# Two global attention steps per batch: all eight heads on half of the keys each, instead of four heads on all keys

## The chip, the cores and the metric

The kernel runs on one core of one Trainium2 chip. The metric is the device time of one execution in microseconds (us), and lower is better. In the rows, PE is TensorE (PEld its weight loads), DVE is VectorE, ACT is ScalarE, POOL is GpSimd and SP is SyncE, which issues most transfers.

## The reference

Local and global attention, then a layer of one expert that takes the 128 highest-scoring tokens of each batch. Cut to what matters:

```python
batch, n_heads, seq_l, seq_g, head_dim = (8, 8, 512, 32, 64)
...
def sm(s):
    s = s - np.max(s, axis=-1, keepdims=True)
    e = np.exp(s)
    return e / (np.sum(e, axis=-1, keepdims=True) + 1e-09)
k_all = np.concatenate([k_g, k_l], axis=2)
v_all = np.concatenate([v_g, v_l], axis=2)
s_g = scale * np.matmul(q_g, k_all.transpose(0, 1, 3, 2))
out_g = np.matmul(sm(s_g), v_all)
...
mask = np.abs(pos[:, None] - pos[None, :]) <= window      # window = 32
s_l = np.concatenate([s_lg, s_ll], axis=-1)
out_l = np.matmul(sm(s_l), np.concatenate([v_g, v_l], axis=2))
x = np.concatenate([out_g, out_l], axis=2)                # to (B, 544, 512)
...
scores = np.einsum('bsd,d->bs', x, w_gate)
top_idx = np.argpartition(-scores[b], capacity)[:capacity]    # per batch
ye = np.maximum(xe @ w1, 0.0) @ w2                            # xe = x[b, top_idx]
out[b, top_idx] = x[b, top_idx] + g[:, None] * ye             # g = sigmoid(scores)
```

The change is in `s_g` and `out_g`: 32 global queries in each of 8 heads, against 544 keys, in each of 8 batches.

## The kernel before, in words

A batch is six steps, in the order L0, L1, G0, G1, L2, L3. A local step (L) takes 128 local queries of all eight heads against their windows of 128 keys. A global step (G) takes the 32 global queries of four heads against all 544 keys, so that heads times queries fill the 128 partitions. There are 48 steps, and one loop writes their instructions out; each engine runs its own list in that written order, so the order in the code is the order on the engine.

One turn of the loop, for step i, does the following.

- PE: for local steps `opened` of step i+1 (a matmul that writes the mask, L209); the attend matmuls of step i-1 (L284 for L, L378 for G); the score matmuls of step i+1 (L228 for L, L337 for G); the transposes of step i's probabilities (L267 for L, L368 for G); then a portion of the expert's matmuls, the fill (L510, L538, L554), whose size a planner sets.
- DVE: `attend_out` of step i-1 (L299, L301, L306 for L; L388, L390, L392 for G), the row maxima of step i+1 (L240 for L; L341, L342, L344 for G), the gate score of a finished tile (L323), then its share of the ranking of the batch before (L424, L426, L434, L436), one or two tiles of tokens per turn, and the second halves of the expert's products (L541).
- ACT: the copies of step i's transposed probabilities from PSUM to SBUF (`turned`, L272), then the scaling of step i+1's maxima (L248) and its exponentials (L258 for L, L352 for G), then the expert's copies and relus (L540).

So the exponentials of step i+1 follow its scores and maxima in the same turn, and its transposes come one turn later. In G steps the probabilities go to the tile `pg`, whose blocks that no key uses are zeroed once at the start. The score tiles `s_ps` are PSUM banks, two to a step, from a pool of six; a step's banks come free when `attend_out` has read the result.

Every matmul in float32 stands in the trace as two matmuls and two weight loads. Score matmuls use a quarter of the array's columns (32 queries) and half of its rows (64 of the head dimension): heads with an even index take rows 0 to 63, heads with an odd one rows 64 to 127. In L steps a row of the score tile is a chunk of 32 queries, and the two heads of a pair go to the two banks. In G steps before the change head h of four goes to columns 32h of the array, with rows 64 * (h % 2).

K, V and Q come by SP's queue: for each batch four tiles `v_t` (V of 128 local keys and their neighbours, two transfers each), `k_t` and `q_t` tiles, and stores of the result. A wait of SP holds what is written behind it. Each step's global result is written by one transfer of SP (L394), behind L392.

## Time and profile before

| | us |
|---|---|
| three runs, median | 345.84 |
| three runs, lowest and highest | 342.60 and 345.89 |
| the profiled execution | 338.32 |
| its span, first to last instruction | 336.1 |

| engine | busy share of the span |
|---|---|
| PE | 84% |
| PEld | 67% |
| DVE | 64% |
| ACT | 51% |
| POOL | 12% |

The profiled execution took 2.2 us outside its span. It is 7.5 us shorter than the median of the three runs; what is worked out from it is a difference in time, which is then put on the median. Busy shares are means over stages with different limits: the first 80 us also load the expert's weights, the middle is attention with fill, and the last 45 us are the expert's alone. TensorE's granted clock is at full speed (2.4 GHz) for 95% of the span by the mean, and at 1.2 GHz in single slices.

### The profile page before, as it was taken

To read this page: it belongs to the slowest core of one execution; us is meant where nothing else is said; L and a number is where in the kernel's file an instruction comes from. 1 tells how busy PE (TensorE), PEld (TensorE's weight loads), DVE (VectorE), ACT (ScalarE), POOL (GpSimd) and SP (SyncE) were. 2 spreads that over 40 slices of the span, in tenths; PEclk is the share of its full clock that TensorE was granted. 3 is DMA by queue.
4 is the path that set the end of the run, shared out by engine and by line. 5 is a ranking of instruction groups with operands and counts; after the bars stand their busy time and mean duration, and the time that the engine had idled before them with its cause. 6 is when DMAs were issued, how large, how long until landed. Compare 5 with 4: busy or idle time off the path is not lost.

```text
span 336.1 us, 14525 instructions
## 1 busy us (share of the span) xinstructions
PE 282.5 (84%) x6328; PEld 226.7 (67%) x6328; DVE 215.6 (64%) x673; ACT 173.0 (51%) x515; POOL 38.8 (12%) x38
## 2 busy tenths in 40 slices
...
GB/s 216 396 408 387 400 385 403 219 248 393 342 37 72 368 403 185 80 377 410 190 11 346 405 244 62 190 390 406 69 67 377 213 33 31 116 33 29 34 33 31
DMA packets 29951, 75.93 MB, mean 226 GB/s; under 512 B 5440, under 2 KB 9408, under 8 KB 29888
## 3 DMA queue, kind: packets, MB, share of 16 engines
...
q8 instruction: 50, 0.82, 1.0%
q10 hardware_dynamic: 288, 0.15, 0.2%
...
## 4 chain that ended last, share of the span: by engine, by line
PE 44%; issue 20%; DVE 13%; DMA 11%; ACT 8%; POOL 3%; SPq 1%; POOLq 0%; DVEq 0%; ACTq 0%
PE s_ps L284 8%; PE s_ps L267 6%; PE s_ps L228 6%; PE m_ps L554 6%; DMA v_t<-in_vw_dram 5%; PE m_ps L538 5%; ACT p_t L258 5%; PE s_ps L337 4%; DMA k_t<-in_kT_dram 4%; DVE mxl L240 3%; DVE junk L424 2%; PE s_ps L378 2%; DMA xe<-out_dram,ix 2%; PE s_ps L368 2%; DVE junk L426 2%
## 5 line engine op out<-in xcount | busy, mean ns | idle before, releaser
L272 ACT COPY pt<-s_ps 128x512 f32<-128x512 f32 (+1 forms) x96 | 50.5, 556 | 67.6 <-PE s_ps L267 34.0
L258 ACT ACTIVATE p_t<-s_ps,nb 128x128 f32<-128x128 f32 x256 | 69.5, 383 | 1.0
L284 PE MATMUL s_ps<-v_t,pt 128*32 128x65 f32 x2048 | 41.7, 231 | 15.1 <-issue 12.2
L284 PEld LDWEIGHTS s_ps<-v_t,pt 128*32 128x32 f32 x2048 | 34.4, 115 | 24.5 <-issue 17.6
L240 DVE TENSOR_REDUCE mxl<-s_ps 128x4 f32<-128x512 f32 x64 | 41.0, 682 | 10.8 <-PE s_ps L228 10.7
L228 PE MATMUL s_ps<-k_t,q_t 64*32 64x128 f32 x2048 | 41.8, 292 | 5.4 <-issue 2.7
L267 PE MATMUL s_ps<-cs,p_t 128*128 128x128 f32 x256 | 39.0, 295 | 3.6 <-issue 2.0
L228 PEld LDWEIGHTS s_ps<-k_t,q_t 64*32 64x32 f32 x2048 | 31.5, 112 | 10.2 <-issue 7.4
L267 PEld LDWEIGHTS s_ps<-cs,p_t 128*128 128x128 f32 x256 | 29.6, 150 | 11.2 <-issue 6.5
L299 DVE TENSOR_SCALAR den<-s_ps 128x4 f32<-128x4 f32 x64 | 9.1, 157 | 29.1 <-PE s_ps L284 25.3
L424 DVE SCALAR_TENSOR_TENSOR junk<-r,sc,side_w 128x128 bf16<-128x128 f32 (+4 forms) x40 | 24.7, 617 | 1.7 <-ACT r L412 0.2
L306 DVE TENSOR_TENSOR x<-s_ps,rec 128x256 f32<-128x256 f32 x64 | 24.2, 419 | 1.1
L323 DVE CUSTOM_DVE_ANT_0 junk<-x,wgb 128x512 bf16<-128x512 f32 x32 | 23.7, 741 | 0.1
L426 DVE SCALAR_TENSOR_TENSOR junk<-r,sc,side_w 128x544 bf16<-128x544 f32 (+4 forms) x40 | 22.4, 560 | 2.1 <-DMA q_t<-in_qT_dram 0.2
...
L561 POOL DMA_INDIRECT out_dram<-xe,ix x8 | 8.1, 1013 | 117.9 <-DVE recg L390 60.6
L248 ACT ACTIVATE nb<-mxl 128x8 f32<-128x8 f32 x32 | 6.9, 216 | 27.9 <-DVE mxl L240 27.8
L337 PE MATMUL s_ps<-k_t,qg_t 64*32 64x256 f32 (+1 forms) x384 | 20.3, 342 | 0.9 <-DMA qg_t<-in_qgT_dram 0.9
L554 PE MATMUL m_ps<-w2h,hTh 128*128 128x512 f32 x48 | 20.6, 429 | 0.2 <-DVE xe L559 0.2
L538 PE MATMUL m_ps<-xTh,w1h 128*128 128x256 f32 x76 | 19.8, 294 | 0.0
L541 DVE SCALAR_TENSOR_TENSOR hTl<-m_ps,hTh 128x256 fp32r<-128x256 f32 x19 | 8.0, 424 | 17.3 <-ACT hTh L540 17.3
L554 PE MATMUL m_ps<-w2l,hTh 128*128 128x512 f32 x48 | 19.1, 398 | 0.0
...
## 6 DMA issues: line engine op xcount, KB each, us to landing
...
```

Source lines behind the costliest of these rows:

```text
L228: nc.tensor.matmul(out=s_ps[hp][32 * j:32 * j + 32, P * pr:P * pr + P], lhsT=q_t[t // 2][rows, pr, 32 * (c % 8):32 * (c % 8) + 32], rhs=wi ...
L240: nc.vector.tensor_reduce(out=mx[:, NPAIR * hp:NPAIR * hp + NPAIR], in_=s_ps[hp].rearrange("p (r k) -> p r k", k=P), axis=AX.X, op=ALU.max)
L258: nc.scalar.activation(out=p_t[:, cc], in_=s_ps[hp][:, cc], func=AF.Exp, scale=0.125, bias=nb[:, k:k + 1])
L267: nc.tensor.transpose(s_ps[hp][:, cc], p_t[:, cc], ident)
L272: nc.scalar.copy(out=pt[:, 0:n], in_=s_ps[hp][:, 0:n])
L284: nc.tensor.matmul(out=s_ps[hp][32 * j:32 * j + 32, VD * pr:VD * pr + VD], lhsT=pt[:, x0:x0 + 32], rhs=v_t[:, j, NPAIR * hp + pr, :], star ...
L306: nc.vector.tensor_tensor(out=xt[b, t][:, :, hp], in0=o_ps[hp][:, :, 0:D], in1=rec[:, hp].broadcast_to([P, NPAIR, D]), op=ALU.mult)
L337: nc.tensor.matmul(out=s_ps[part][32 * h:32 * h + 32, c0:c1], lhsT=qg_t[rows, pr, :], rhs=r_, start=True, stop=True)
L424: nc.vector.scalar_tensor_tensor(out=junk[:n, 0:hi], in0=r[:n, 0:hi], scalar=s, in1=side_w[:n, P + SL - lo:P + SL - lo + hi], op0=ALU.is_g ...
L426: nc.vector.scalar_tensor_tensor(out=junk[:n, lo:ST], in0=r[:n, lo:ST], scalar=s, in1=side_w[:n, 0:ST - lo], op0=ALU.is_gt, op1=ALU.mult, ...
L538: nc.tensor.matmul(out=h_ps, lhsT=a[:, kc, ms], rhs=xT[x_][:, kc, :], start=(i == 0), stop=(i == len(prods) - 1))
L554: nc.tensor.matmul(out=y_ps, lhsT=hT[h_][:, mc, cc], rhs=w[:, mc, :], start=(part == 0 and i == 0), stop=(part == 3 and i == len(prods) - 1))
```

## The change

Each of the two G steps of a batch now takes all eight heads on half of the keys: step G0 takes 288 key columns, step G1 256. Heads of even index go to one bank (`hp` 0), of odd index to the other (`hp` 1), as in L steps. Each half has its own maximum, so the second step forms the minimum of the two scaled maxima, and a factor `gf` by which the first half's sum is rescaled; `oa` holds that sum in SBUF in between. G0 no longer divides or stores; G1 does it for all eight heads, with one transfer.

The tile `pg` is the same size, split by `hp`; a block that only G0 fills is zeroed by DVE in each G1 (L365 of the changed kernel). ACT has one more exponential, of `gf`, behind those of G1.

```diff
@@ -25,7 +25,6 @@
 NPAIR = H // 2
 NQ = H // 4
 VD = D + 1
-OG = 300
 KB = 3 * (NC // 2) + 2
 KW = 32 * KB
 KW1 = 448
@@ -61,10 +60,9 @@
 
 
 
-_GWIN = (0, 3, 6, 9, 12, 15)
-NGB = 4 * len(_GWIN)
-GH = (2, 4)
-GCOL = (((0, 256, 0),), ((0, 256, 384), (256, 288, 768)))
+GWIN = ((0, 3, 6), (9, 12, 15))
+GN = (288, 256)
+OG = 400
 
 
 @with_exitstack
@@ -146,10 +144,11 @@
                 return ps_s.tile([P, 512], FP32, name="s_ps")
         return ps_m.tile([P, 512], FP32, name="m_ps")
 
-    pg = cst.tile([P, NGB, 32], FP32, name="pg")
-    nc.vector.memset(pg[:, 0:8], 0.0)
-    nc.gpsimd.memset(pg[:, 8:], 0.0)
-    wz = pg[:, 0:8].rearrange("p n k -> p (n k)").bitcast(BF16)
+    pg = cst.tile([P, 2, 12, 32], FP32, name="pg")
+    nc.vector.memset(pg[:, 0, 0:8], 0.0)
+    nc.gpsimd.memset(pg[:, 0, 8:], 0.0)
+    nc.gpsimd.memset(pg[:, 1], 0.0)
+    wz = pg[:, 0, 0:8].rearrange("p n k -> p (n k)").bitcast(BF16)
     for i in range(WARM):
         w_ps = m_tile()
         nc.tensor.matmul(out=w_ps, lhsT=wz[:, 0:P], rhs=wz, start=True, stop=True)
@@ -234,7 +233,7 @@
 
     def maxima(g, s_ps):
         if g[1] == "G":
-            return g_max(s_ps)
+            return g_max(g[0], g[2], s_ps)
         mx = sm.tile([P, H], FP32, name="mxl")
         for hp in range(2):
             nc.vector.tensor_reduce(out=mx[:, NPAIR * hp:NPAIR * hp + NPAIR], in_=s_ps[hp].rearrange("p (r k) -> p r k", k=P),
@@ -250,7 +249,7 @@
 
     def expo(g, s_ps, nb, hp):
         if g[1] == "G":
-            return g_exp(s_ps[hp], nb, hp)
+            return g_exp(g[2], s_ps[hp], nb, hp)
         p_t = att.tile([P, 512], FP32, name=f"p_t{hp}")
         for pr in range(NPAIR):
             cc = slice(P * pr, P * pr + P)
@@ -268,14 +267,14 @@
 
     def turned(g, s_ps, hp):
         pt = att.tile([P, 512], FP32, name=f"pt{hp}")
-        n = GH[hp] * P if g[1] == "G" else 512
+        n = 3 * P if g[1] == "G" else 512
         nc.scalar.copy(out=pt[:, 0:n], in_=s_ps[hp][:, 0:n])
         return pt
 
     def attend_mm(g, pt, s_ps, hp):
         b, kind, t = g
         if kind == "G":
-            g_attend(b, t, pt, s_ps[0], hp)
+            g_attend(b, t, pt, s_ps[hp], hp)
             return
         v_t = vts[b, t]
         for pr in range(NPAIR):
@@ -291,7 +290,7 @@
     def attend_out(g, s_ps):
         b, kind, t = g
         if kind == "G":
-            g_out(b, t, s_ps[0])
+            g_out(b, t, s_ps)
             return
         o_ps = [s_[:, 0:NPAIR * VD].rearrange("p (r d) -> p r d", d=VD) for s_ in s_ps]
         den = sm.tile([P, 2, NPAIR, 1], FP32, name="den")
@@ -325,73 +324,101 @@
             scale=1.0, scalar=0.0, accum_out=dst,
         )
 
-    def g_scores(b, hq, s_ps):
+    def g_scores(b, part, s_ps):
         _, k_t, qg_t = loaded[b]
-        for part in range(2):
-            for h in range(4):
-                pr = 2 * hq + h // 2
-                rows = slice(D * (h % 2), D * (h % 2) + D)
-                kk = k_t[rows, pr, :]
-                for c0, c1, x0 in GCOL[part]:
-                    r_ = kk[:, x0:x0 + 384].rearrange("p (a x) -> p a x", x=96)[:, :, 0:64] if c1 - c0 > 32 else kk[:, x0:x0 + 32]
-                    nc.tensor.matmul(out=s_ps[part][32 * h:32 * h + 32, c0:c1], lhsT=qg_t[rows, pr, :], rhs=r_, start=True, stop=True)
-
-    def g_max(s_ps):
+
+        def run(c0, n, dstep, x0, xstep, ln):
+            for pr in range(NPAIR):
+                for hp in range(2):
+                    rows = slice(D * hp, D * hp + D)
+                    o_ = s_ps[hp][32 * pr:32 * pr + 32, c0:c0 + ln]
+                    k_ = k_t[rows, pr, x0:x0 + ln]
+                    nc.tensor.matmul(
+                        out=bass.AP(tensor=o_.tensor, offset=o_.offset, ap=[o_.ap[0], [dstep, n], [1, ln]]),
+                        lhsT=qg_t[rows, pr, :],
+                        rhs=bass.AP(tensor=k_.tensor, offset=k_.offset, ap=[k_.ap[0], [xstep, n], [1, ln]]),
+                        start=True, stop=True)
+
+        if part == 0:
+            run(0, 4, 64, 0, 96, 64)
+            run(256, 1, 32, 32 * 12, 32, 32)
+        else:
+            run(32, 3, 64, 32 * 15, 96, 64)
+            run(0, 2, 224, 32 * 13, 32 * 11, 32)
+
+    gs = {}
+
+    def g_max(b, part, s_ps):
         mx = sm.tile([P, 2], FP32, name="mx")
-        nc.vector.tensor_reduce(out=mx[:, 0:1], in_=s_ps[0][:, 0:256], axis=AX.X, op=ALU.max)
-        nc.vector.tensor_reduce(out=mx[:, 1:2], in_=s_ps[1][:, 0:288], axis=AX.X, op=ALU.max)
-        nb = sm.tile([P, 1], FP32, name="nbg")
-        nc.vector.tensor_scalar(out=nb, in0=mx[:, 0:1], scalar1=mx[:, 1:2], scalar2=-0.125, op0=ALU.max, op1=ALU.mult)
+        for hp in range(2):
+            nc.vector.tensor_reduce(out=mx[:, hp:hp + 1], in_=s_ps[hp][:, 0:GN[part]], axis=AX.X, op=ALU.max)
+        nb = sm.tile([P, 2], FP32, name="nbg")
+        if part == 0:
+            nc.vector.tensor_scalar(out=nb, in0=mx, scalar1=-0.125, scalar2=None, op0=ALU.mult)
+            gs[b] = [nb]
+        else:
+            na = gs[b][0]
+            nc.vector.scalar_tensor_tensor(out=nb, in0=mx, scalar=-0.125, in1=na, op0=ALU.mult, op1=ALU.min)
+            gf = sm.tile([P, 2], FP32, name="gf")
+            nc.vector.tensor_tensor(out=gf, in0=nb, in1=na, op=ALU.subtract)
+            gs[b].append(gf)
+            nc.vector.memset(pg[:, :, 11], 0.0)
         return nb
 
-    def g_exp(s_ps, nb, hp):
-        bv = s_ps.rearrange("p (n k) -> p n k", k=32)
+    def g_exp(part, s_ps, nb, hp):
+        bv = s_ps[:, 0:288].rearrange("p (n k) -> p n k", k=32)
 
         def run(src, dst, n, ln):
-            s_, d_ = bv[:, src], pg[:, dst]
+            s_, d_ = bv[:, src], pg[:, hp, dst]
             nc.scalar.activation(
                 out=bass.AP(tensor=d_.tensor, offset=d_.offset, ap=[d_.ap[0], [4 * 32, n], [1, 32 * ln]]),
                 in_=bass.AP(tensor=s_.tensor, offset=s_.offset, ap=[s_.ap[0], [3 * 32, n], [1, 32 * ln]]),
-                func=AF.Exp, scale=0.125, bias=nb)
-
-        if hp == 0:
-            run(0, 0, 1, 2)
-            run(2, 3, 2, 3)
-        else:
-            run(0, 11, 3, 3)
-        return pg
+                func=AF.Exp, scale=0.125, bias=nb[:, hp:hp + 1])
+
+        run(0, 0, 1, 2)
+        run(2, 3, 2, 3)
+        if part == 0:
+            run(8, 11, 1, 1)
+        return pg[:, hp]
 
     def g_transp(pg, s_ps, hp):
         pf = pg.rearrange("p n k -> p (n k)")
-        for i in range(GH[hp]):
-            x0 = P * (GH[0] * hp + i)
-            nc.tensor.transpose(s_ps[:, P * i:P * i + P], pf[:, x0:x0 + P], ident)
+        for n in range(3):
+            nc.tensor.transpose(s_ps[:, P * n:P * n + P], pf[:, P * n:P * n + P], ident)
 
     xg = {}
 
-    def g_attend(b, hq, ptg, s_ps, hp):
+    def g_attend(b, part, ptg, s_ps, hp):
         og = s_ps[:, OG:OG + VD]
-        for n in range(GH[hp]):
-            i = GH[0] * hp + n
-            c = _GWIN[i]
-            for h in range(4):
+        for n in range(3):
+            c = GWIN[part][n]
+            for pr in range(NPAIR):
                 nc.tensor.matmul(
-                    out=og[32 * h:32 * h + 32, :],
-                    lhsT=ptg[:, P * n + 32 * h:P * n + 32 * h + 32],
-                    rhs=vts[b, c // 4][:, c % 4, NPAIR * (h % 2) + 2 * hq + h // 2, :],
-                    start=(i == 0), stop=(i == len(_GWIN) - 1),
+                    out=og[32 * pr:32 * pr + 32, :],
+                    lhsT=ptg[:, P * n + 32 * pr:P * n + 32 * pr + 32],
+                    rhs=vts[b, c // 4][:, c % 4, NPAIR * hp + pr, :],
+                    start=(n == 0), stop=(n == 2),
                 )
 
-    def g_out(b, hq, s_ps):
-        og = s_ps[:, OG:OG + VD]
-        den = sm.tile([P, 1], FP32, name="deng")
-        nc.vector.tensor_scalar(out=den, in0=og[:, D:VD], scalar1=1e-9, scalar2=None, op0=ALU.add)
-        rec = sm.tile([P, 1], FP32, name="recg")
+    def g_out(b, part, s_ps):
+        if part == 0:
+            oa = sm.tile([P, 2, VD], FP32, name="oa", bufs=1)
+            for hp in range(2):
+                nc.vector.tensor_copy(out=oa[:, hp], in_=s_ps[hp][:, OG:OG + VD])
+            gs[b].append(oa)
+            return
+        _, gf, oa = gs.pop(b)
+        for hp in range(2):
+            nc.vector.scalar_tensor_tensor(out=oa[:, hp], in0=oa[:, hp], scalar=gf[:, hp:hp + 1],
+                                           in1=s_ps[hp][:, OG:OG + VD], op0=ALU.mult, op1=ALU.add)
+        den = sm.tile([P, 2, 1], FP32, name="deng")
+        nc.vector.tensor_scalar(out=den, in0=oa[:, :, D:VD], scalar1=1e-9, scalar2=None, op0=ALU.add)
+        rec = sm.tile([P, 2, 1], FP32, name="recg")
         nc.vector.reciprocal(out=rec, in_=den)
-        ogs = sm.tile([P, D], FP32, name="ogs")
-        nc.vector.tensor_scalar(out=ogs, in0=og[:, 0:D], scalar1=rec, scalar2=None, op0=ALU.mult)
-        dst = outs[b][0:SG, 4 * D * hq:4 * D * hq + 4 * D].rearrange("g (h d) -> h g d", d=D)
-        nc.sync.dma_start(out=dst, in_=ogs)
+        ogs = sm.tile([P, 2, D], FP32, name="ogs", bufs=2)
+        nc.vector.tensor_tensor(out=ogs, in0=oa[:, :, 0:D], in1=rec.broadcast_to([P, 2, D]), op=ALU.mult)
+        dst = outs[b][0:SG, :].rearrange("g (r x) -> r g x", x=2 * D)
+        nc.sync.dma_start(out=dst, in_=ogs.rearrange("p a d -> p (a d)"))
 
     def load_xg(b):
         xg[b] = xp.tile([SG, DM], FP32, name="xg")
@@ -725,6 +752,9 @@
             NB = bias(work[i + 1], MX.pop(i + 1))
             for hp in range(2):
                 PR[hp] = expo(work[i + 1], S[i + 1], NB, hp)
+            if work[i + 1][1:] == ("G", 1):
+                gf = gs[b][1]
+                nc.scalar.activation(out=gf, in_=gf, func=AF.Exp)
         if i == nstep:
             run_stores()
         if i == LATE:
```

What this does to the lists of three engines, at the places that the prediction speaks of (lines in the second fence of each pair are those of the changed kernel).

On ACT, the two G steps of the second batch, from the copies of L1's probabilities (`pt`) to those of G0's, before and then now:

```order
L272 COPY pt_958<-s_ps 128x512
L272 COPY pt_960<-s_ps 128x512
L352 ACTIVATE pg<-s_ps,nbg 128x64
L352 ACTIVATE pg<-s_ps,nbg 128x2x96
L352 ACTIVATE pg<-s_ps,nbg 128x3x96
L190 CAST w1h<-hTh 128x512 x2
L272 COPY pt_1040<-s_ps 128x256
L272 COPY pt_1042<-s_ps 128x512
```

The three exponentials of G0 stand ahead of the expert's work (here a cast of its weights). Now:

```order
L271 COPY pt_977<-s_ps 128x512
L271 COPY pt_979<-s_ps 128x512
L373 ACTIVATE pg<-s_ps,nbg 128x64
L373 ACTIVATE pg<-s_ps,nbg 128x2x96
L373 ACTIVATE pg<-s_ps,nbg 128x32
L373 ACTIVATE pg<-s_ps,nbg 128x64
L373 ACTIVATE pg<-s_ps,nbg 128x2x96
L373 ACTIVATE pg<-s_ps,nbg 128x32
L189 CAST w1h<-hTh 128x512 x2
L271 COPY pt_1069<-s_ps 128x384
L271 COPY pt_1071<-s_ps 128x384
```

There are six exponentials where there were three, and the expert's work is behind all six; the two copies are of equal width.

On DVE, in the second batch, from the last of the ranking (`oh` is its result) through G1's `attend_out` to L3's maxima (`mxl`), before:

```order
L434 TENSOR_TENSOR rank<-cnt 128x5
L436 TENSOR_TENSOR oh<-slot_119,rank 128x640
L388 TENSOR_SCALAR deng<-s_ps 128x1
L390 RECIPROCAL recg<-deng 128x1
L392 TENSOR_SCALAR ogs<-s_ps,recg 128x64
L240 TENSOR_REDUCE mxl<-s_ps 128x4 x2
```

L3's maxima stand behind three small instructions. Now:

```order
L461 TENSOR_TENSOR rank<-cnt 128x5
L463 TENSOR_TENSOR oh<-slot_120,rank 128x640
L412 SCALAR_TENSOR_TENSOR oa<-oa,gf,s_ps 128x65 x2
L415 TENSOR_SCALAR deng<-oa 128x2
L417 RECIPROCAL recg<-deng 128x2
L419 TENSOR_TENSOR ogs<-oa,recg 128x128
L239 TENSOR_REDUCE mxl<-s_ps 128x4 x2
```

They stand behind five, two of which read PSUM.

On PE, the attend matmuls of G0 in the first batch with their waits (DMAHW is a transfer, here of `v_t` tiles), before:

```order
L378 MATMUL s_ps<-v_t,pt_422 32x65 [waits Activation_49]
L378 MATMUL s_ps<-v_t,pt_422 32x65 x7
L378 MATMUL s_ps<-v_t,pt_424 32x65 [waits Activation_49]
L378 MATMUL s_ps<-v_t,pt_424 32x65 x3
L378 MATMUL s_ps<-v_t,pt_424 32x65 [waits DMAHW6_49]
L378 MATMUL s_ps<-v_t,pt_424 32x65 x3
L378 MATMUL s_ps<-v_t,pt_424 32x65 [waits DMAHW0_49]
L378 MATMUL s_ps<-v_t,pt_424 32x65 x3
L378 MATMUL s_ps<-v_t,pt_424 32x65 [waits DMAHW1_49]
L378 MATMUL s_ps<-v_t,pt_424 32x65 x3
L228 MATMUL s_ps<-k_t,q_t 32x128 [waits DMAHW5_49]
```

G0 waits for the third and fourth `v_t` tiles. Now:

```order
L396 MATMUL s_ps<-v_t,pt_437 32x65 [waits Activation_49]
L396 MATMUL s_ps<-v_t,pt_437 32x65 x11
L396 MATMUL s_ps<-v_t,pt_439 32x65 [waits Activation_49]
L396 MATMUL s_ps<-v_t,pt_439 32x65 x11
L227 MATMUL s_ps<-k_t,q_t 32x128 [waits DMAHW5_49]
```

The three waits for transfers have moved to G1's attend matmuls, one turn later; the count of attend matmuls is the same.

## Rows read from the trace of the kernel before

**Rows 1.** The page: busy time of each engine; the chain, by engine and line

```profile
PE 282.5 (84%) x6328; PEld 226.7 (67%) x6328; DVE 215.6 (64%) x673; ACT 173.0 (51%) x515; POOL 38.8 (12%) x38
...
PE 44%; issue 20%; DVE 13%; DMA 11%; ACT 8%; POOL 3%; SPq 1%; POOLq 0%; DVEq 0%; ACTq 0%
PE s_ps L284 8%; PE s_ps L267 6%; PE s_ps L228 6%; PE m_ps L554 6%; DMA v_t<-in_vw_dram 5%; PE m_ps L538 5%; ACT p_t L258 5%; PE s_ps L337 4%; DMA k_t<-in_kT_dram 4%; DVE mxl L240 3%; DVE junk L424 2%; PE s_ps L378 2%; DMA xe<-out_dram,ix 2%; PE s_ps L368 2%; DVE junk L426 2%
```

**Rows 2.** The chain in order of time: start, length, what (score matmuls)

```profile
49.46 1.45 PE s_ps L337 x20
...
163.44 1.10 PE s_ps L337 x20
...
167.80 1.09 PE s_ps L228 x64
...
190.57 1.98 PE s_ps L337 x24
...
264.66 1.52 PE s_ps L337 x20
```

**Rows 3.** Window: stretch, its length, busy us of each engine, PEclk, DMA, GB/s

```profile
190.60:192.50 1.90, 1.90 (x25) 0.91 (x25) 0.82 (x3) 0.43 (x2) 0.00 (x0) 0.50 1.05 411
```

**Rows 4.** Groups by form, ACT's exponentials of G steps: busy, mean ns, idle before

```profile
L352 ACT ACTIVATE pg<-s_ps,nbg 128x288 f32<-128x288 f32 x16 | 8.2, 515 | 0.0
...
L352 ACT ACTIVATE pg<-s_ps,nbg 128x192 f32<-128x192 f32 x16 | 6.8, 427 | 0.0
...
L352 ACT ACTIVATE pg<-s_ps,nbg 128x64 f32<-128x64 f32 x16 | 5.2, 324 | 0.1
```

**Rows 5.** Groups by form, DVE: instructions like the new ones

```profile
L306 DVE TENSOR_TENSOR x<-s_ps,rec 128x256 f32<-128x256 f32 x64 | 24.2, 419 | 1.1
...
L541 DVE SCALAR_TENSOR_TENSOR hTl<-m_ps,hTh 128x256 fp32r<-128x256 f32 x19 | 8.0, 424 | 17.3 <-ACT hTh L540 17.3
...
L392 DVE TENSOR_SCALAR ogs<-s_ps,recg 128x64 f32<-128x64 f32 x16 | 4.5, 284 | 0.6
```

**Rows 6.** The chain in the third batch, 96 to 110 us

```profile
104.28 0.67 PE s_ps L267 x4
...
104.95 0.16 DVE deng L388
...
105.34 0.28 DVE ogs L392
...
105.62 1.19 DVE mxl L240 x2
```

**Rows 7.** Timeline, sixth batch, L3: start, length, engine, line

```profile
212.01 1.28 DVE L240 TENSOR_REDUCE mxl<-s_ps 128x4 f32<-128x512 f32 x2
...
213.56 2.17 ACT L258 ACTIVATE p_t<-s_ps,nb 128x128 f32<-128x128 f32 x8
...
215.62 1.09 PE L267 MATMUL s_ps<-cs,p_t 128*128 128x128 f32 x8
```

**Rows 8.** Timeline, fifth batch, G0's exponentials and what stands behind them

```profile
157.27 1.03 ACT L352 ACTIVATE pg<-s_ps,nbg 128x64 f32<-128x64 f32 x3
158.16 0.41 ACT L540 ACTIVATE hTh<-m_ps 128x256 fp32r<-128x256 f32 x1
...
158.61 0.42 DVE L541 SCALAR_TENSOR_TENSOR hTl<-m_ps,hTh 128x256 fp32r<-128x256 f32 x1 [0.16 <-ACT hTh L540]
...
159.38 0.28 PE L538 MATMUL m_ps<-xTh,w1h 128*128 128x256 f32 x1
```

**Rows 9.** Timeline, PE in the first batch: idle time before in brackets

```profile
24.36 0.32 PE L378 MATMUL s_ps<-v_t,pt 128*32 128x65 f32 x8 [0.97 <-DMA v_t<-in_vw_dram]
...
39.53 1.64 PE L284 MATMUL s_ps<-v_t,pt 128*32 128x65 f32 x58 [3.01 <-issue]
```

**Rows 10.** DMA queues from 36 to 40 us: packets, MB, share of 16 engines

```profile
q1 hardware_dynamic: 748, 1.60, 103.3%
q8 instruction: 1, 0.02, 1.5%
```

## Prediction

> **What bounds the kernel now.** The page comes first. PE is busy for 84% of the span, yet only 44% of the chain that ended last is PE's; 20% is "issue", 13% DVE, 11% DMA and 8% ACT [rows 1]. So no engine is the bound throughout, and the reader should ask of each stretch which of these ends last. The global scores (L337) hold 4% of the chain, 4% of 336.1 = 13.4 us. The chain in order of time says where: eleven of the sixteen G steps are on it, eight of them at 1.10 us, three longer, at 1.45, 1.98 and 1.52 us [rows 2]. In the longest the granted clock was 0.50, the 1.2 GHz level [rows 3].
>
> Then the same chain, asked for a part of the span only. In the third batch it leaves PE: the transposes of L2 end, then DVE's three small instructions of G1's result and the maxima of L3 follow one another [rows 6]. In the sixth batch, which has more fill, the path stays on PE, but with little room: L3's transposes run from 215.62 for 1.09 us, so their second half is due at 216.17, and the exponentials it needs end at 213.56 + 2.17 = 215.73, 0.44 earlier [rows 7]. Last, the first batch: PE stops for 3.01 us in the middle of one run of attend matmuls, with "issue" as the reason [rows 9]. In those four microseconds the data queue fills the DMA engines and one instruction packet moves [rows 10]; I read it as PE waiting for its own instructions behind data.
>
> **The scores.** Before, a G step's eight 256-column and four 32-column matmuls use four quarters of the array's columns, each with one half of its rows: four places. Each place streams 2 x (256 + 256 + 32) = 1088 columns (every float32 matmul runs twice) in 1.10 us, about 1.0 ns a column [rows 2]. After, the eight heads lie on all eight places, as local scores do. There a place streams 8 x 128 = 1024 columns in 1.09 us, 1.06 ns a column, so eight places side by side run at nearly the rate of four [rows 2]. G0 has 2 x (256 + 32) = 576 columns a place, 0.58 to 0.61 us; G1 has 512, 0.51 to 0.54. The gain is about 0.5 us in G0 and 0.55 in G1, twice that at the low clock. If every piece on the chain were halved, 13.4 us would lose 6.7.
>
> **ACT.** G0's three exponentials cost 324 + 427 + 515 = 1266 ns by their means, and 1.03 us from first to last since they overlap [rows 4, 8]. The six after are twice 324 + 427, and two of 32 columns. No row has that size; by the line through the three, about 300 each. That is 2.1 us by means, and about 1.7 from first to last: 0.7 more. G1's four are 1.5 us, 0.24 more, and the new exponential of the factor, bounded by zero and the 324 of the 64-column one, stands behind them; I take 0.2. All this lies beside PE's fill unless the next ACT work feeds PE. In the fifth batch it does: the relu at 158.16 waits behind G0's exponentials, DVE's L541 (158.61 + 0.42 = 159.03) behind the relu, and PE's third group, at 159.38, needs the bank that both free, 0.35 us of room [rows 8]. With the exponentials 0.7 longer, PE waits about 0.35 there, and it arrives 0.5 earlier thanks to the scores. The net gain of G0 is then some 0.1, and I take that for the three batches whose fill has an ACT copy there, the fourth, fifth and seventh.
>
> **DVE.** Maxima keep their sizes in sum. New in G1 are three small instructions for two (0.27 us: a second scaled minimum, the difference, and the zeroing of a block). The zeroing waits for PE's transposes of G0, written just behind the scores that the maxima wait for; the two reductions ahead of it cover them. Without that cover the local score and the ranking behind it on DVE would stand still for the transposes, under 1 us. In G0 two copies of 65 columns replace three dependent instructions (0.67 us from L388 to L240 [rows 6]): I take 0.2 less. In G1 five instructions replace three. The two that read PSUM lie between a fitted 0.18 (L541's 424 ns is for 256 columns) and L392's 284 each; the 128-column product between L392's 284 and L306's 419 at most, and it reads SBUF [rows 5]. I take 1.1 us for the five, against 0.67: 0.45 more, with ends of 0.2 and 0.9. So L2's maxima come 0.1 later and L3's 0.55, measured from the local result of L1.
>
> **V and the first batch.** G0's wait of 0.97 us for `v_t` [rows 9] goes, since G0 now uses the first two tiles. What is late next is PE's instructions, for which the first batch's runs of attend matmuls stop again and again, as in the row of 3.01 us. A packet arrives when the data ahead of it has passed, so PE gets no earlier to the end of what it has. It gets there with less done, since each G step has four more matmuls, 16 entries of PE's list. I take 0.4 us of loss for the batch; the ends are a gain of 1.0 (the wait counts in full) and a loss of 0.8.
>
> The Trainium skill, "Runtime: NRT & Kernel Launch", section "Instruction fetch mechanics", says that an engine's instructions stream in blocks of 16 KiB and that crossing from one block to the next is mostly hidden. By that the first batch would keep its 1.0 us, and the sum below would be a gain of 1.6 us rather than of 0.2. The idle of 3.01 us amid a run of matmuls without any wait speaks against it here.
>
> **Edits at nothing.** Transposes, attend matmuls and copied columns are equal in number. SP issues one store fewer per batch; the loads behind it were held by G1's store before and still are, which now comes 0.45 us later with DVE. PE reaches those loads' data two steps later, which covers it. POOL's memset at the start is as long as before.
>
> **The sum,** as the shift that each batch hands on. First batch +0.4. In the second, third, fourth and eighth, whose path I take through DVE to L3's exponentials, G1's 0.55 us on PE only turns into waiting, and the shift is 0.55 less G0's gain: 0.55 - 0.7 (1.45 us halved), 0.55 - 0.5, 0.55 - 0.1, 0.55 - 0.75 (1.52 halved). In the fifth, sixth and seventh, which have as much fill, I take the room of 0.4 us that the sixth shows [rows 7], so 0.15 less G0's gain: 0.15 - 0.1, 0.15 - 1.0 (1.98 halved), 0.15 - 0.1. In all 0.4 - 0.15 + 0.05 + 0.45 - 0.2 + 0.05 - 0.85 + 0.05 = -0.2 us, 338.1 for the profiled execution of 338.3. The median of the runs is 345.84, 7.5 above it; put on the median, 345.6. The three runs differ by 3.3 us, so I take 1%, 3.4 us, as what can be told from no change.
>
> **The rivals.** First, PE is the bound and DVE and ACT have room: all eleven pieces halve, 345.8 - 6.7 = 339.1. For it speak PE's 84% and the unbroken PE path of the sixth batch; against it, the DVE pieces of the third and the 0.44 us of [rows 7]. Second, slower: G1's result on DVE costs its upper end, 0.9 instead of 0.45, and G0's longer exponentials hold PE's fill in all of the seven later batches, so that G0's gain, 3.25 us in the sum above, is lost too. Then the sum is -0.2 + 7 x 0.45 + 3.25 = 6.2, 352.0. It decides from the point at which DVE's added work before L3's maxima exceeds the room that PE's fill leaves; for it speaks that DVE is on the chain for 13%, against it that fill varies from batch to batch. Third, the change doesn't do what it says: the two heads that share a quarter of the columns run one behind the other. Then scores take 1.1 us as before, the same 3.25 us go, and the time is 345.6 + 3.3 = 348.9; local scores, which pair heads so, speak against it.
>
> Beside all of them stands the shuffle of "issue" idles. The added entries move the points at which PE runs out of instructions, and one such idle is worth up to 3 us, and more where PE's clock drops behind it [rows 3, 9]. It has no sign, and I widen the range by it.
>
> **How the numbers follow.** The forecast of no change gets 0.47, the first rival 0.28, the second 0.17, the third 0.08. The forecast's own range is 341.5 to 349.5 from the ends of the DVE price, the first batch and one idle. The whole range goes down to 338.5, just under the first rival, and up to 350.5, short of the second's end; that leaves out some 2 in 10. Faster by over 1% (under 342.4): the first rival and a twelfth of the forecast, 0.32. Slower by over 1% (over 349.3): most of the second rival, some of the third and of the forecast, 0.21. Within 1%: 0.47.
>
> **What would show it.** Scores of a G step near 0.6 us show the first part; 1.1 would show the third rival. G0's six exponentials should span about 1.7 us, and DVE's five instructions 1.1 before L3's maxima. If PE then waits for ACT ahead of L3's transposes in most batches, the gain went where I say; if those transposes follow PE's own work without idle, the first rival holds. PE's "issue" idle in all, 20% of the chain now, should stay within some 5 us; a larger move would make the sum moot. The forecast is wrong if DVE's stretch from L1's result to L3's maxima is not longer than before, or if the path no longer runs through it.

## The result and the profile after

The changed kernel takes 345.69 us (median of 20 runs, 341.44 to 349.54), the kernel before 342.69 on the same chip (20 runs, 336.98 to 349.63): a ratio of 1.0118, 95% interval 1.007 to 1.0165, 4.0 us slower by the ratio and 3.0 by the medians. The forecast was no change. The time lies inside its range, but the change is a loss. That the forecast's 345.6 us is so near is luck: it was put on a median of three runs, 345.84, which lies 3.15 above that of the 20.

Single runs of one kernel differ by up to 4% here, apart from one run of 623.25 us of the kernel before. The ratios are taken from the undisturbed runs alone; where I compare two experiments of this text, I use the difference of each one's median to the kernel before in its set. Resampled from the runs on record, such a difference is uncertain by 2 to 4 us (95%). So one alone does not settle a question of that size; the ratios or the timelines have to agree with it.

The page of the changed kernel, its busy row, the two rows of its chain:

```profile
PE 283.1 (82%) x6456; PEld 228.3 (66%) x6456; DVE 220.1 (64%) x697; ACT 177.7 (52%) x555; POOL 38.9 (11%) x39
...
PE 35%; DVE 22%; issue 21%; DMA 8%; ACT 8%; POOL 2%; SPq 1%; POOLq 0%; DVEq 0%; ACTq 0%
PE s_ps L283 8%; PE s_ps L266 5%; ACT p_t L257 5%; DVE junk L451 5%; PE s_ps L227 5%; DVE mxl L239 4%; PE m_ps L565 4%; PE m_ps L581 3%; DVE junk L453 3%; DMA v_t<-in_vw_dram 3%; PE s_ps L336 2%; DMA xe<-out_dram,ix 2%; DMA xg<-out_dram 2%; ACT pt L271 2%; DVE x L305 2%
```

Against [rows 1] PE fell from 44% to 35% of the chain and DVE rose from 13% to 22%: where PE got shorter, DVE took its place (37% and 20% in a second profile of the changed kernel, the run c_after below). The scores (L336) fell from 4% to 2%. PE has 128 matmuls and 128 weight loads more, 256 entries of its list.

The timelines of the third batch show that the parts have the sizes that were forecast, first PE's, then ACT's:

```profile
94.43 0.72 PE L336 MATMUL s_ps<-k_t,qg_t 64*32 64x256 f32 x32
...
99.99 0.67 PE L336 MATMUL s_ps<-k_t,qg_t 64*32 64x192 f32 x32
100.59 0.88 PE L387 MATMUL s_ps<-cs,pg 128*128 128x128 f32 x6
```

```profile
96.74 1.51 ACT L373 ACTIVATE pg<-s_ps,nbg 128x64 f32<-128x64 f32 x6
...
102.62 1.14 ACT L373 ACTIVATE pg<-s_ps,nbg 128x64 f32<-128x64 f32 x4 [0.53 <-DVE pg L365]
103.63 0.22 ACT L757 ACTIVATE gf<-gf 128x2 f32<-128x2 f32 x1
```

The next instruction starts 0.66 and 0.60 us after the start of the scores of G0 and G1 (1.10 before, [rows 2]). G0's exponentials take 1.51 us. They begin at 96.74 and the transposes that need them at 100.59: PE's fill covers them with 2.3 us to spare. G1's first exponential waits for DVE's zeroing of `pg`, which was not forecast.

DVE's timeline of the same batch, where [rows 6] stood before:

```profile
109.48 0.82 DVE L463 TENSOR_TENSOR oh<-slot,rank 128x640 f16<-128x640 f16 x1
110.22 0.47 DVE L412 SCALAR_TENSOR_TENSOR oa<-oa,gf,s_ps 128x65 f32<-128x65 f32 x2
110.72 0.17 DVE L415 TENSOR_SCALAR deng<-oa 128x2 f32<-128x2 f32 x1
110.93 0.17 DVE L417 RECIPROCAL recg<-deng 128x2 f32<-128x2 f32 x1
111.12 0.29 DVE L419 TENSOR_TENSOR ogs<-oa,recg 128x128 f32<-128x128 f32 x1
111.33 1.28 DVE L239 TENSOR_REDUCE mxl<-s_ps 128x4 f32<-128x512 f32 x2
```

Five instructions take 1.11 us, from 110.22 to the maxima at 111.33. No row has an idle in brackets: DVE comes to G1's result straight from the ranking of the batch before (the one-hot of L463 ends it) and has been busy since L2's maxima. So what G1's result takes more, L3's maxima come later, in full. The time from L2's maxima to L3's, read from the starts of these instructions in DVE's timeline (us):

| batch | 3 | 4 | 5 | 6 | 7 | 8 |
|---|---|---|---|---|---|---|
| before | 5.04 | 5.05 | 5.37 | 5.66 | 5.37 | 6.16 |
| after | 5.57 | 5.57 | 5.90 | 6.18 | 5.90 | 6.68 |

The difference is 0.52 or 0.53 in every one. The step from G1's maxima to L2's is 0.13 to 0.22 shorter in five of the six batches, 0.43 in the last (G0's two copies instead of three instructions). Together, from G1's maxima to L3's, the changed kernel is 0.40, 0.34, 0.34, 0.30, 0.34 and 0.09 us longer, 1.8 in the six batches. What PE waits for tells the same (engine, tile and line, what it waited for: us in all, times, longest), after and then before:

```profile
PE s_ps L266 <- ACT p_t L257: 7.2, 10, 2.3
```

```profile
PE s_ps L267 <- ACT p_t L258: 1.5, 4, 0.5
```

In the sixth batch, where the path stayed on PE before [rows 7], the chain of the changed kernel runs through DVE, from the ranking to G1's result:

```profile
217.55 0.18 DVE rank L461
...
219.19 0.40 DVE oa L412 x2
...
220.01 0.30 DVE ogs L419
```

In the second profile (c_after) it leaves PE only at L2's transposes, and then passes through the same instructions to L3's maxima:

```profile
214.39 0.60 PE s_ps L266 x4
...
215.67 0.40 DVE oa L412 x2
...
216.71 1.29 DVE mxl L239 x2
```

The first batch. PE's timeline, of the changed kernel:

```profile
18.88 0.66 PE L336 MATMUL s_ps<-k_t,qg_t 64*32 64x192 f32 x30
22.59 0.37 PE L336 MATMUL s_ps<-k_t,qg_t 64*32 64x64 f32 x2 [3.05 <-issue]
22.89 1.54 PE L387 MATMUL s_ps<-cs,pg 128*128 128x128 f32 x6
...
24.79 1.53 PE L396 MATMUL s_ps<-v_t,pt 128*32 128x65 f32 x48
26.24 1.96 PE L227 MATMUL s_ps<-k_t,q_t 64*32 64x128 f32 x64
```

And of the kernel before, at the same stop:

```profile
19.97 0.87 PE L368 MATMUL s_ps<-cs,pg 128*128 128x128 f32 x6
...
22.60 0.79 PE L378 MATMUL s_ps<-v_t,pt 128*32 128x65 f32 x35 [1.31 <-issue]
```

Both go on at 22.6, and the wait for `v_t` of [rows 9] is gone (24.79 has none). But the stop now falls two matmuls ahead of the end of G1's scores, before it fell into G0's attend matmuls. So at 22.6 the changed kernel has G0's transposes still to do, and behind the longer idle it does them in 1.54 us instead of 0.87.

The granted clock tells why the pieces got longer. From 22.6 to 29.0 us, now and then before (stretch, its length, busy us of PE, PEld, DVE, ACT and POOL, PEclk, DMA, GB/s):

```profile
22.60:29.00 6.40, 6.40 (x128) 5.20 (x128) 2.63 (x10) 2.13 (x8) 0.00 (x0) 0.53 1.03 402
```

```profile
22.60:29.00 6.40, 3.84 (x145) 3.00 (x148) 1.90 (x5) 2.67 (x10) 0.00 (x0) 1.00 1.03 403
```

Behind the stop of 3.05 us the clock is at its lower level (1.2 GHz) for nearly all of this stretch; before, it was at full speed. (The mean of 0.95 in the description of the kernel before is a mean of the two levels: 90% of its span was at full speed, not 95%.) The second batch begins with L0's maxima, now and before:

```profile
39.31 1.29 DVE L239 TENSOR_REDUCE mxl<-s_ps 128x4 f32<-128x512 f32 x2 [0.43 <-PE s_ps L227]
```

```profile
35.09 1.28 DVE L240 TENSOR_REDUCE mxl<-s_ps 128x4 f32<-128x512 f32 x2
```

That is 4.2 us later, and 3.3 in c_after (38.38): as much as the whole loss. These are single executions, but the others agree in the main. In the profiles of e1, e2, e3, e6, e7, f1 and f5 below, whose PE lists are about as long as the changed kernel's, the second batch begins between 37.6 and 39.0; in e4, e5, e9, e10, f3 and f4, with a shorter list, between 35.6 and 37.6. Length alone does not decide it: b2 and f6, with the long list, are at 34.3 and 35.6, and b1, with the list of the kernel before, is at 38.2.

### The profile page after: what moved, and what is told of

Its sections match the earlier page's. It is cut to its first block, busy times and chain, and to the rows that moved or that the text cites. A ratio compares the mean times of both kernels' runs of the same rounds, so it can differ in the third digit from the quotient of the medians.

```text
span 344.1 us, 14845 instructions
## 1 busy us (share of the span) xinstructions
PE 283.1 (82%) x6456; PEld 228.3 (66%) x6456; DVE 220.1 (64%) x697; ACT 177.7 (52%) x555; POOL 38.9 (11%) x39
## 4 chain that ended last, share of the span: by engine, by line
PE 35%; DVE 22%; issue 21%; DMA 8%; ACT 8%; POOL 2%; SPq 1%; POOLq 0%; DVEq 0%; ACTq 0%
PE s_ps L283 8%; PE s_ps L266 5%; ACT p_t L257 5%; DVE junk L451 5%; PE s_ps L227 5%; DVE mxl L239 4%; PE m_ps L565 4%; PE m_ps L581 3%; DVE junk L453 3%; DMA v_t<-in_vw_dram 3%; PE s_ps L336 2%; DMA xe<-out_dram,ix 2%; DMA xg<-out_dram 2%; ACT pt L271 2%; DVE x L305 2%
## 5 line engine op out<-in xcount | busy, mean ns | idle before, releaser
L271 ACT COPY pt<-s_ps 128x512 f32<-128x512 f32 (+1 forms) x96 | 49.6, 558 | 65.9 <-PE s_ps L266 34.7
L283 PE MATMUL s_ps<-v_t,pt 128*32 128x65 f32 x2048 | 44.0, 238 | 12.4 <-issue 9.8
L283 PEld LDWEIGHTS s_ps<-v_t,pt 128*32 128x32 f32 x2048 | 36.3, 120 | 22.0 <-issue 15.1
L227 PE MATMUL s_ps<-k_t,q_t 64*32 64x128 f32 x2048 | 43.8, 294 | 6.3 <-issue 4.1
L266 PE MATMUL s_ps<-cs,p_t 128*128 128x128 f32 x256 | 38.8, 293 | 12.1 <-ACT p_t L257 7.2
L266 PEld LDWEIGHTS s_ps<-cs,p_t 128*128 128x128 f32 x256 | 29.3, 148 | 19.4 <-ACT p_t L257 10.7
L227 PEld LDWEIGHTS s_ps<-k_t,q_t 64*32 64x32 f32 x2048 | 32.5, 113 | 12.3 <-issue 10.1
L451 DVE SCALAR_TENSOR_TENSOR junk<-r,sc,side_w 128x128 bf16<-128x128 f32 (+4 forms) x40 | 25.4, 636 | 1.7 <-ACT r L439 0.2
L453 DVE SCALAR_TENSOR_TENSOR junk<-r,sc,side_w 128x544 bf16<-128x544 f32 (+4 forms) x40 | 21.5, 538 | 2.0
L373 ACT ACTIVATE pg<-s_ps,nbg 128x64 f32<-128x64 f32 (+2 forms) x80 | 21.2, 366 | 1.6 <-DVE nbg L361 1.0
L322 DVE CUSTOM_DVE_ANT_0 junk<-x,wgb 128x512 bf16<-128x512 f32 x32 | 21.7, 677 | 0.1
L565 PE MATMUL m_ps<-xTh,w1h 128*128 128x256 f32 x76 | 20.3, 298 | 0.3 <-DVE hTl L568 0.3
```

Source lines behind the costliest of these rows:

```text
L227: nc.tensor.matmul(out=s_ps[hp][32 * j:32 * j + 32, P * pr:P * pr + P], lhsT=q_t[t // 2][rows, pr, 32 * (c % 8):32 * (c % 8) + 32], rhs=wi ...
L266: nc.tensor.transpose(s_ps[hp][:, cc], p_t[:, cc], ident)
L271: nc.scalar.copy(out=pt[:, 0:n], in_=s_ps[hp][:, 0:n])
L283: nc.tensor.matmul(out=s_ps[hp][32 * j:32 * j + 32, VD * pr:VD * pr + VD], lhsT=pt[:, x0:x0 + 32], rhs=v_t[:, j, NPAIR * hp + pr, :], star ...
L322: nc.vector.tensor_tensor_reduce(out=junk[:n, 0:DM], in0=xf, in1=wgb[:n], op0=ALU.mult, op1=ALU.add, scale=1.0, scalar=0.0, accum_out=dst,)
L451: nc.vector.scalar_tensor_tensor(out=junk[:n, 0:hi], in0=r[:n, 0:hi], scalar=s, in1=side_w[:n, P + SL - lo:P + SL - lo + hi], op0=ALU.is_g ...
```

## The experiments

Three theories stood against each other. **D**: DVE's added work around G1 is on the path. **A**: ACT's exponentials are. **S**, later **P**: PE's list of instructions, longer by 256, and the places where it stops, are.

| kernel | median, us (runs) | to before, us | ratio, 95% |
|---|---|---|---|
| changed, again (c_after) | 343.59 (12) | +3.0 | 1.0027 (0.9973 to 1.0082) |
| e1: no zeroing | 342.59 (12) | +2.0 | 1.0007 (0.9952 to 1.0061) |
| e2: short result of G1 | 340.06 (7) | -0.5 | 0.9867 (0.9786 to 0.9949) |
| e3: two exponentials | 341.79 (12) | +1.2 | 1.0111 (1.0044 to 1.0178) |
| e6: maxima first | 346.67 (6) | +5.5 | 1.0342 (1.0162 to 1.0521) |
| b1: before, maxima first | 342.91 (6) | +1.7 | 1.0204 (1.0015 to 1.0393) |
| e7: scores alone | 338.40 (6) | -2.8 | 1.0135 (0.9994 to 1.0276) |
| e4: one run of scores | 339.64 (6) | -1.6 | 1.0103 (0.9847 to 1.0358) |
| b2: before, sixteen matmuls | 340.71 (12) | +0.6 | 1.0005 (0.9941 to 1.0068) |
| e5: e1 and e4 | 339.28 (12) | -0.8 | 0.9978 (0.9928 to 1.0027) |
| e9: e5, sum on PE | 333.79 (6) | -6.3 | 0.9861 (0.9791 to 0.9932) |
| e10: e9, one exponential in G1 | 334.02 (6) | -6.1 | 0.9784 (0.9671 to 0.9897) |
| f1: two warm-up matmuls | 342.70 (6) | +1.9 | 1.0124 (1.0052 to 1.0197) |
| f3: e5, long scores | 340.64 (12) | -0.2 | 1.0082 (1.0034 to 1.0130) |
| f4: e9, long scores | 335.60 (7) | -5.2 | 0.9854 (0.9768 to 0.9940) |
| f5: e5, two runs of scores | 343.47 (12) | +2.8 | 1.0057 (0.9999 to 1.0115) |
| f6: e9, two runs of scores | 340.33 (6) | -0.3 | none |

The medians before lie between 340.11 and 341.21. The ratios of e4, e6, e7 and b1 rest on two of the eleven runs of the kernel before in their set, 332.29 and 336.98, which are the fastest there, and may all be too high. Those of e4 and e7 point the other way than their medians; nothing below rests on these four alone.

**Three parts taken away, one at a time.** The control, then e1:

> The changed kernel as it is, beside the next three on one chip. Three theories of its loss of 1.2% (4.0 us): D, DVE's added work around G1 (the zeroing and the five instructions of the result) lies on the path; A, ACT's additional exponentials lie on it; S, the loss is in PE's instruction list, which got longer, and in where it stops. All expect a ratio of 1.012 again, within 1.007 to 1.017.

```diff
-            nc.vector.memset(pg[:, :, 11], 0.0)
+    vw[:, NT - 1, 96:P, 3] = 0.0
```

The added line is in the layout of V.

> The changed kernel without DVE's zeroing of a block of pg in each G1: that block keeps G0's numbers, and the rows of V that it meets are zeros in the input's layout, so the result is unchanged. G1's exponentials then wait for the bias only, not for the zeroing behind it and with it for PE's transposes of G0. D: 0.1 to 0.3 us less in each of the eight batches and 0.8 more in the first, where the zeroing waited 0.80 us: 1.6 to 3.2 us less than the changed kernel, ratio to the kernel before 1.003 to 1.007. A and S: within 0.5 us of the changed kernel.

The control is 3.0 above the kernel before again, by its median; its ratio is lower than the first one, the two intervals overlap, and its own holds no change. Without the zeroing 1.0 goes, less than D's 1.6 and too little to be sure of. Then e2:

```diff
-            nc.vector.scalar_tensor_tensor(out=oa[:, hp], in0=oa[:, hp], scalar=gf[:, hp:hp + 1], ...
-        nc.vector.tensor_scalar(out=den, in0=oa[:, :, D:VD], ...
+        nc.vector.tensor_scalar(out=den, in0=s_ps[1][:, OG + D:OG + VD], ...
```

> The changed kernel with G1's result made by three short DVE instructions instead of five: the two that add the rescaled first half to the second are left out, so the global rows of the output lack the second half of the keys. D: DVE's stretch ahead of L3's maxima falls from 1.1 to about 0.6 us in each batch, 8 x 0.5 = 4 us less if it all lies on the path, ratio 1.000; half of it, 1.006. A and S: within 0.5 us of the changed kernel, 1.010 to 1.012.

3.5 us less than the control of its set, as D says, and the intervals of the two ratios lie apart. Its steps from L2's maxima to L3's are those of the kernel before to 0.01 us (5.04, 5.04, 5.37, 5.65, 5.37, 6.15), and the five instructions' 1.11 became 0.59:

```profile
109.49 0.15 DVE L412 TENSOR_SCALAR deng<-s_ps 128x1 f32<-128x1 f32 x1
109.68 0.16 DVE L414 RECIPROCAL recg<-deng 128x1 f32<-128x1 f32 x1
109.87 0.29 DVE L416 TENSOR_SCALAR ogs<-oa,recg 128x128 f32<-128x128 f32 x1
110.08 1.28 DVE L239 TENSOR_REDUCE mxl<-s_ps 128x4 f32<-128x512 f32 x2
```

e3:

```diff
-        run(0, 0, 1, 2)
-        run(2, 3, 2, 3)
...
+        nc.scalar.activation(out=pg[:, hp, 0:n], in_=bv[:, 0:n], func=AF.Exp, scale=0.125, bias=nb[:, hp:hp + 1])
```

> The changed kernel with one exponential for each half of the heads in a G step (288 or 256 columns) instead of three or two: the blocks land side by side, so the probabilities of the global rows meet the wrong rows of V. A: G0's exponentials fall from 1.5 us to about 1.0 and G1's from 1.14 to 1.0, some 0.6 us a batch, up to 5 us less, ratio 1.000 or below. D and S: under 1 us, ratio 1.009 to 1.012.

G0's exponentials fell from 1.51 to 0.91 us and G1's from 1.14 to 0.84; the median is 1.8 below the control's, the ratio above it (1.0111, the control 1.0027). By the median at most a part of A's 5 us is there, by the ratio nothing, which agrees with the cover of 2.3 us seen above.

**The order on DVE turned round.** In e6 and b1:

```diff
-        if i > 0:
+        if i > 0 and work[i - 1][1] == "L":
             attend_out(work[i - 1], S.pop(i - 1))
         if i + 1 < nstep:
             MX[i + 1] = maxima(work[i + 1], S[i + 1])
+        if i > 0 and work[i - 1][1] == "G":
+            attend_out(work[i - 1], S.pop(i - 1))
```

> The changed kernel with one order turned round on DVE: where the step before was a global one, the maxima of the next step are written ahead of that global result instead of behind it (L2's maxima ahead of G0's two copies and of nothing else, L3's ahead of G1's five instructions). D (DVE is packed with ranking when it comes to G1's result, so all five instructions delay L3's maxima): L3's maxima come 1.1 us earlier in the seven batches that carry ranking, L2's 0.27, 5 to 9 us less than the changed kernel if PE then has nothing else to wait for, half of that if L3's transposes run into the fill: ratio to the kernel before 0.985 to 1.0. A and S: within 1 us of the changed kernel, 1.006 to 1.012.

> The kernel before with the same order turned round: the maxima of the step behind a global one are written ahead of that global result. Its results are three instructions, 0.67 us, in G0 and in G1. D: L2's and L3's maxima each come 0.67 us earlier where DVE is packed, 3 to 7 us less than the kernel before, ratio 0.98 to 0.991. A and S: within 1 us of the kernel before. If this gains as much as the same turn does in the changed kernel, the order and not the change is what it pays for.

A miss for all theories. e6 is 2.5 us above the changed kernel by the medians; b1 did not gain, and its 1.7 us above the kernel before are within the noise. What the masks of L steps (L208) waited for in e6, us and times:

```profile
  DVE oa L407: 5.7, 5
  DVE oa L412: 4.8, 7
```

In the changed kernel that is 1.7 us, once. The maxima do come earlier (L2's to L3's 4.72 instead of 5.57 in the third batch). But a G step's banks come free when its result has been read, and the step that opens next needs them; the later result holds the mask on PE, and all behind it. In e6 that takes back what the order gives. In b1 the masks' wait for G's result is that of the kernel before (5.4 us, 5.5 before), so why b1 gains nothing stays open.

**The scores alone, and the length of PE's list.** e7 takes e1, e2 and e3 together and the minimum, difference and factor away:

> The changed kernel with all that the running maximum and the new halves add left out: no minimum and difference, no zeroing, no factor's exponential, one exponential for each half of the heads, G1's result from three short instructions of G0's sum. The global rows of the output are not the reference's. What is left is the scores on eight places. D and A with a gain of the scores on PE as forecast: 3 to 6 us below the kernel before, ratio 0.982 to 0.991. If the scores' gain is lost elsewhere (the whole loss is in PE's list, S): ratio 1.0 or above.

The median is 2.8 below the kernel before, just under what was expected, and 5.8 below the changed kernel; the ratio, 1.0135, would be S's. Its steps from G1's maxima to L2's are 0.40 to 0.49 shorter than before, 2.55 us in the last six batches, those from L2's to L3's equal. So most of what it gains by the median over the kernel before, too, is found in steps that DVE fills. e4 and b2:

```diff
-        if part == 0:
-            run(0, 4, 64, 0, 96, 64)
-            run(256, 1, 32, 32 * 12, 32, 32)
...
+        run(0, 5, 64, 32 * 12 * part, 96, 64)
```

> The changed kernel with eight score matmuls of 320 columns in each G step instead of sixteen (256 and 32, or 192 and 2 x 32): some columns are computed twice and not used further, the result is unchanged. PE's list has 256 matmuls and weight loads fewer of each kind over the batches, and each place streams 640 columns instead of 576 and 512. S (the longer list costs the changed kernel its gain): 2 to 4 us less than the changed kernel, ratio 1.0 to 1.006. D and A: PE has 0.05 and 0.1 us more in the two steps, no change to 1.5 us more, ratio 1.010 to 1.016.

```diff
-GCOL = (((0, 256, 0),), ((0, 256, 384), (256, 288, 768)))
+GCOL = (((0, 128, 0), (128, 256, 192)), ((0, 256, 384), (256, 288, 768)))
```

> The kernel before with sixteen score matmuls in each G step instead of twelve: each 256-column one of the first bank is split into two of 128. Columns, places and everything on DVE and ACT are as before; PE's list is as long as the changed kernel's. S (the length of PE's list): 2 to 4 us more than the kernel before, ratio 1.006 to 1.012. D and A: 0 to 1 us more, ratio 0.998 to 1.003.

By the medians they contradict each other on S: the shorter list gives 4.6, the longer one costs 0.6. In b2's first batch PE stops at the same place as the changed kernel, two matmuls ahead of the end of G1's scores, but for 1.21 us, up to 21.33, and the clock stays at full speed. e5 agrees with e4, at 3.8 us below the changed kernel:

> The changed kernel with both earlier edits that leave the result unchanged: no zeroing in G1, and eight score matmuls of 320 columns in a G step. If the two medians seen (1.0 us less without the zeroing, 4 us less with the shorter list, both against the changed kernel) hold and add, the ratio is 0.994 to 0.998. If the shorter list's gain was chance (D and A), 1.006 to 1.010.

**The result summed on PE.** e9, on top of e5:

```diff
+            nc.tensor.matmul(out=s_ps[:, OG:OG + 2 * VD], lhsT=ident, rhs=gs[b][2].rearrange("p a d -> p (a d)"),
+                             start=True, stop=False, skip_group_check=True)
...
-                nc.vector.tensor_copy(out=oa[:, hp], in_=s_ps[hp][:, OG:OG + VD])
+            nc.vector.scalar_tensor_tensor(out=oa, in0=og, scalar=1e-9, in1=gf.broadcast_to([P, 2, VD]), op0=ALU.add, op1=ALU.mult)
...
+        nc.vector.reciprocal(out=rec, in_=og[:, :, D:VD])
```

> The last kernel with the two halves added by PE: the results of both halves of the heads go to one bank, DVE rescales G0's sum in one instruction as it copies it out of PSUM, PE adds it to G1's in one matmul with the identity, and G1's result is two DVE instructions instead of five. The result is unchanged. D: L2's maxima to L3's fall from 5.82 us to about 5.2, below the 5.30 of the kernel before, in the batches that carry ranking; 3 to 4 us less than the kernel without this edit. A and S: within 0.5 us of it.

By the medians 5.5 us less than e5, more than D's 3 to 4; by the ratio 1.4% below the kernel before. DVE's timeline:

```profile
104.54 0.82 DVE L456 TENSOR_TENSOR oh<-slot,rank 128x640 f16<-128x640 f16 x1
105.29 0.16 DVE L410 RECIPROCAL recg<-s_ps 128x2 f32<-128x2 f32 x1
105.48 0.29 DVE L412 TENSOR_TENSOR ogs<-s_ps,recg 128x128 f32<-128x128 f32 x1
105.69 1.28 DVE L239 TENSOR_REDUCE mxl<-s_ps 128x4 f32<-128x512 f32 x2
```

0.40 us ahead of L3's maxima, 0.71 less than the changed kernel; its steps from L2's maxima to L3's are 4.85, 4.85, 5.19, 5.47, 5.19 and 5.98, and PE's wait for ACT ahead of L266 is 2.0 us (4.5 in e5, 7.2 in the changed kernel). e10 adds

```diff
+            run(0, -1, 3, 3)
```

for G1's two runs of exponentials:

> The last kernel with one exponential for each half of the heads in G1 instead of two: the three groups of three blocks go out in one instruction of 288 columns, whose first block is a key that G0 has already and lands beside the blocks in use. The result is unchanged. A: G1's exponentials fall from 1.14 us to about 0.9; 0 to 1.5 us less than the kernel without this edit. D and S: within 0.5 us of it.

G1's exponentials fell from 1.14 to 0.89 us and the median did not move (0.2 up, the ratio lower): again nothing for A.

**What the shorter scores give, and what the list is worth.** f3 and f4 lengthen the scores to what they were, with `run(0, 8, 64, 96 * part, 96, 64)`; f1 sets `WARM` from 8 to 2:

> The changed kernel with two warm-up matmuls at the start instead of eight, which nothing reads: PE's list is 12 entries shorter ahead of everything else, so each point at which PE stops for its next instructions lies 12 entries later in the program. In the first batch the stop of 3.05 us, which falls two matmuls before the end of G1's scores, then falls behind four of G0's six transposes; G1's maxima and exponentials run during it. P (where the stops fall costs the changed kernel its first batch, about 2 us, and 1 to 2 us in the fourth): 1 to 3 us less than the changed kernel, ratio to the kernel before 1.001 to 1.006. D alone: within 0.5 us of the changed kernel, 1.008 to 1.012. The cold start may cost up to 1 us at TensorE's lower clock.

> The kernel with one run of scores and no zeroing, its eight score matmuls of 512 columns instead of 320: a G step's scores take about 1.2 us again, as in the kernel before, and everything else and the number of instructions stay; the result is unchanged. If the scores' gain lies on the path, 16 x 0.43 = 6.9 us more than with 320 columns, or half of it, 3.4, ratio 1.008 to 1.018. If DVE's ranking and PE's other waits hide it (D), 0 to 1.5 us more, ratio 0.997 to 1.003.

> The same lengthening of the scores in the kernel whose halves are added by PE, where DVE has less to do at G1's result (ratio 0.986 without the lengthening). If DVE's added work was what hid the scores' gain, the longer scores now cost 3 to 7 us, ratio 0.995 to 1.007. If they are hidden here too, 0 to 1.5 us, ratio 0.984 to 0.991.

In f3 the scores of both steps take 1.09 us, 0.77 in e5:

```profile
124.75 1.09 PE L336 MATMUL s_ps<-k_t,qg_t 64*32 64x512 f32 x16
130.43 1.09 PE L336 MATMUL s_ps<-k_t,qg_t 64*32 64x512 f32 x16
```

By the medians that costs 0.6 us without and 1.1 with the sum on PE, of 5.1 that it would cost on the path (16 x 0.32; the 0.43 of the expectation was too much). By the ratios f3 costs 3.5 against e5 (1.0082 less 0.9978, of 340), and f4 nothing against e9 (0.9854 and 0.9861). So by the medians about a fifth or less of the scores' length is on the path, by f3's ratio two thirds: how much stays open. For G1's scores the timelines settle it. The step from G0's maxima to G1's is the same to 0.03 us in f4 and e9 in seven batches, and shorter in f4 in the eighth, and DVE comes to G1's maxima without idle time in all of them. f1 moved the stop of the first batch behind G1's scores as meant, and gave 1.1 by its median and nothing by its ratio: not settled. f5 and f6 split the one run of scores in two, same columns, PE's list as long as the changed kernel's (6456 matmuls, against 6200 in e5):

```diff
-        run(0, 5, 64, 32 * 12 * part, 96, 64)
+        run(0, 3, 64, 32 * 12 * part, 96, 64)
+        run(192, 2, 64, 32 * (12 * part + 9), 96, 64)
```

> The kernel with one run of scores and no zeroing, its eight matmuls of 320 columns split into sixteen of 192 and 128: the same columns, but PE's list is as long as the changed kernel's again and its stops fall where they fall there. The result is unchanged. P (the list and where its stops fall are what the one run of scores gains, some 3 us): ratio 1.004 to 1.010. If the list does not matter: within 1 us of the kernel it is made from, 0.995 to 1.002.

> The same split in the kernel whose halves are added by PE (ratio 0.986 without it). P: about 3 us more, ratio 0.993 to 0.998. If the list does not matter: within 1 us, 0.983 to 0.990.

3.6 and 6.0 us more by the medians, for 512 entries more in PE's list and the same columns: P by its sign in both kernels, and by its size or more. It is not beyond doubt. The intervals of e5 and f5 overlap a little, and f6's six runs spread from 332.08 to 344.68 us and give no ratio. Much of it shows in the fourth batch, on PE, at L1's attend matmuls. f5 stops there:

```profile
122.16 0.24 PE L283 MATMUL s_ps<-v_t,pt 128*32 128x65 f32 x1 [0.24 <-ACT pt L271]
124.77 1.13 PE L283 MATMUL s_ps<-v_t,pt 128*32 128x65 f32 x63 [2.37 <-issue]
```

e5 does not:

```profile
119.38 0.63 PE L227 MATMUL s_ps<-k_t,q_t 64*32 64x128 f32 x22 [0.37 <-issue]
119.94 1.09 PE L266 MATMUL s_ps<-cs,p_t 128*128 128x128 f32 x8
121.28 1.17 PE L283 MATMUL s_ps<-v_t,pt 128*32 128x65 f32 x64 [0.24 <-ACT pt L271]
```

The changed kernel stops at the same matmuls as f5, for 2.13 us. In this batch the step from L1's maxima to G0's takes 7.3 us in f5, 3.9 in e4 and e5, 6.2 and 7.7 in the two profiles of the changed kernel, 5.4 in the kernel before.

## Why the prediction was wrong, by its own steps

Two terms of the sum failed: the **first batch**, taken as 0.4 us of loss, and **G0's gain of 3.25 us**, taken as gone through.

- **The first batch** had ends of -1.0 and 0.8. The mechanism (PE gets no earlier to its next instructions and has less done) is what the rows at 22.59 show; the size was far too small. The second batch begins 4.2 and 3.3 us later in the two profiles. The stop is 3.05 us instead of 1.31, and the lower clock behind it, which the term did not have, makes 1.54 and 1.96 us of pieces of 0.87 and 1.16. How much of this is the place of the stop is open: b2 stops at the same place for 1.21 us, and its second batch begins at 34.3.
- **The scores on PE** were right in size (0.60 to 0.66 us against the 0.51 to 0.61 taken). The step that failed is the next one: that **G0's 0.5 us goes through**, 3.25 us in the sum. I took the chain's pieces for the price of removing them. f3 and f4 put 0.32 us back in each of the 16 steps: 0.6 and 1.1 us by the medians, at most 3.5 by a ratio.
- **G1's result on DVE** was right in size (1.11 against 1.1, 0.52 more against 0.45), and for the batches whose path I took through DVE. It failed in the **room of 0.4 us in the fifth to seventh batch**, which I had from PE's side [rows 7]: the time between L2's and L3's maxima there is DVE's own, packed with ranking, and grew by 0.53, 0.52 and 0.53. In the fourth batch 0.5 came back in the next step (2.93 to 2.43 us from L3's maxima to the next batch's).
- **L2's maxima** came 0.13 us or more earlier, not 0.1 later. G0's two copies take 0.27 us (105.50 to 105.77) against 0.67 for the three instructions: 0.40 less, where I took 0.2. With the last point this error cancels, by luck: from G1's maxima to L3's the last six batches lost 1.8 us, and the sum had 2.1 for them (three times 0.55 and three times 0.15).
- **The exponentials** had about the sizes taken (1.51 against 1.7, 0.22 against 0.2). That ACT's 0.7 would eat G0's gain in three batches is not shown: in the third batch PE's fill covers the exponentials with 2.3 us to spare, and by the medians e3 leaves 1.8 us in all for the whole of A.
- **The zeroing** stood still for PE's transposes in the first batch only (0.80 us); in the seven later ones the cover held. What I did not see is that G1's exponentials wait for it (0.53 us in the row at 102.62); about 1 us in all by e1.
- What I called a **shuffle without a sign** has one by f5 and f6, if their medians hold: 512 entries cost 3.6 us or more, so in proportion, an estimate, 256 would cost some 1.8. Yet b2's 256 cost the kernel before 0.6 (its interval holds 1.8), and PE's stops over 0.5 us are fewer and shorter in sum in the changed kernel (22.7 us before, 21.6 and 20.3 after).

The parts do not close. By the profiles the changed kernel's span is 8.0 us longer in one and 3.1 in the other. 4.2 and 3.3 of that are there when the second batch begins, and 1.8 is DVE's. What is left, a loss of 2.0 in one and a gain of 2.0 in the other, holds the scores' gain, the later stops and the difference between executions, which these runs do not separate. The second rival had the right mechanism, DVE's added work beyond PE's room, at the forecast's own price instead of its upper end; the first batch supplied the rest.
